# Half of the MLP's down tiles leave PSUM by ScalarE and are summed in DRAM by GpSimd's accumulating DMAs

## The chip, the cores and the metric

One core of a Trainium2 chip. The metric is the device time of one execution in microseconds; the time of a kernel is the median over its runs.

## The reference

With x of 2048 tokens x 576 channels in fp32, two branches are computed and added to x:

```
xn  = layernorm(x)
A   = attention(xn @ wqkv) @ wo        # 32 heads of 18; each token looks at itself and
                                       # 7 earlier tokens, 2 apart (window 8, dilation 2)
h   = gelu(layernorm(xn) @ w1)
hs  = shift(h) @ w2                    # four channel groups shifted by +1, -1, +2, -2 tokens
x1  = xn + hs
B   = x1 + gelu(layernorm(x1) @ w3) @ w4   # w3: 576 x 4608, w4: 4608 x 576
out = x + A + B
```

GELU is the tanh form. Everything has to come out at fp32 accuracy.

## The kernel before, in words

All matmuls run in the fp32r type. Each operand is split into a high and a low part (`split_w`, `split_x`: ScalarE makes the high part by a cast, VectorE the low part by a subtraction), and a product is made of high x high, high x low and low x high. So the 576 input channels become the 14 pairs of 128 rows in `PAIRS`.

The program is written out by hand in one order for each engine. `Y`, 16 tiles of 128 tokens x 576 in SBUF, holds xn, then x1, then the running sum. The stages are: the qkv projection (q, k and v are spilled to DRAM), the token mixing with w1 and w2, the MLP with attention beside it, and at the end the output projection with wo.

The MLP is a loop over 72 units `(c, b)`: 18 chunks of 256 hidden channels, and in each of them 4 blocks of 512 tokens. In a unit stand two up tiles, `up(c, b, i)`, 14 matmuls each into a PSUM bank (L676; two such buffers), and then the four down tiles of the unit before, `down(*prev, j)`, 12 matmuls each into a pair of banks (L696; three such buffers, taken in turn). After an up tile ScalarE passes over it twice with GELU, once to `hi` (rounded to fp32r, L680) and once to `g32` (L681), and VectorE makes `lo = g32 - hi` (L682). After a down tile VectorE adds the PSUM pair to `Y[:, t, :]` (L699). Tile t is 4 b + j.

Attention's vector work has no matmuls. It is a generator (`attention`), and `bg(r)` takes some of its VectorE operations (L628, L631, L608, L612) ahead of each up and down tile, by a budget in microseconds that is written in the code, until all is done; what is left at unit 66 is issued there at once. Its sums are written to `od` in DRAM. Between units 4 and 66 `load_xa` and `add_x` add the input x to `Y`, one tile in four units (L757). The weights of the next chunk are loaded by SP into `rawf` and split by `split_w3` and `split_w4` (L167 on ScalarE, L168 on VectorE).

In the last six units (z = u - 72 = -6 to -1) attention's result comes back: `load_o` loads 512 tokens of `od` in four DMAs (L738), `o_turn` transposes them on VectorE (L129, L130), `put` writes them to DRAM (L137, four DMAs), `get` reads them back with the channels on the partitions (L142), and `split_x` splits them. `load_wo` and `split_wo` do the same for wo. After the loop stand the last four down tiles, and then the output projection, tile by tile (L846), with an add to `Y` (L847) and a store (L848).

Every engine works its instructions off in order; SP issues all DMAs in one queue. GpSimd has nothing to do in the loop.

Of the kernel before, what the change touches and what calls it, by code (L numbers as in the profile page):

```python
# [8 lines left out]
F32 = mybir.dt.float32  # L9
F32R = mybir.dt.float32r  # L10
AF = mybir.ActivationFunctionType
ALU = mybir.AluOpType
# [4 lines left out]
S, D, F = 2048, 576, 4608  # L17
NT = S // 128
NB = S // 512
# [9 lines left out]
NCH = NF // C  # L29
HF = D // 2  # L30
# [10 lines left out]
def dram_ap(t, offset, dims):  # L41
    return bass.AP(tensor=t.tensor, offset=t.offset + offset, ap=[list(d) for d in dims])
# [3 lines left out]
def fused_block(ctx, tc, x, wqkv, wo, w1, w2, w3, w4, out):  # L46
    nc = tc.nc
    pe, act, dve, pool, sp = nc.tensor, nc.scalar, nc.vector, nc.gpsimd, nc.sync
# [8 lines left out]
    dram = ctx.enter_context(tc.tile_pool(name="dram", bufs=1, space=DRAM))  # L57

    Y = base.tile([128, NT, D], F32, name="Y")
# [10 lines left out]
    od = dram.tile([S, D], F32, name="od")  # L70
# [56 lines left out]
    def turn(src, t):  # L127
        c = slice(32 * t, 32 * t + 32)
        dve.transpose(ST[:, 4:20, c], src[:, :512].rearrange("p (j c) -> p j c", c=32))  # L129
        dve.transpose(ST[:, 0:4, c].rearrange("p (a j) c -> p a j c", a=2),  # L130
                      src[:, 512:].rearrange("p (j c) -> p j c", c=32)[:, None, :, :]
                      .to_broadcast([128, 2, 2, 32]))

    def put(key):
        xd[key] = dram.tile([5, 128, 512], F32, name="xd", bufs=4)
        for q in range(4):
            sp.dma_start(dram_ap(xd[key], 128 * q, [[512, 32], [32 * 512, 20], [1, 128]]),  # L137
                         ST[32 * q:32 * q + 32])

    def get(key, xt):  # L140
        for k in ((0, 3), (3, 5)):
            sp.dma_start(xt[:, 4 + k[0]:4 + k[1], :].bitcast(F32),  # L142
                         xd[key][k[0]:k[1]].rearrange("k p c -> p k c"))
# [13 lines left out]
    def in_order(blk):  # L157
        return blk.rearrange("p (q t c) -> p t q c", q=4, t=4)

    def by_token(blk):  # L160
        return blk.rearrange("p (t q c) -> p t q c", q=4, t=4)

    def quads(t_, b, q):
        return dram_ap(t_, (512 * b + 128 * q) * D, [[D, 32], [32 * D, 4], [1, D]])

    def split_w(dst_hi, dst_lo, raw):
        act.copy(dst_hi, raw)  # L167
# [353 lines left out]
    def n_turn(t, zpool):  # L521
        z = zpool.tile([128, D], F32, name="rz", tag="rz")
        act.activation(z, Y[:, t, :], AF.Identity, bias=RS[2][:, t, 0:1], scale=RS[2][:, t, 1:2])  # L523
        turn(z, t % 4)
        if t % 4 == 3:
            put(("n", t // 4))
# [5 lines left out]
    for t in range(NT):  # L532
        ps = psb.tile([128, 2, 512], F32, name="ps", tag="b")
# [9 lines left out]
        yv = Y[:, t, :].rearrange("p (h c) -> p h c", h=2)  # L543
        dve.tensor_tensor(yv, ps[:, :, :HF], yv, op=ALU.add)
        stats(Y[:, t, :], 2, t)
        if t in (1, 3):
            f = (t - 1) // 2
# [22 lines left out]
    hp = ctx.enter_context(tc.tile_pool(name="hp", bufs=2, reuse_waits="tile"))  # L570
    tp = ctx.enter_context(tc.tile_pool(name="tp", bufs=1, reuse_waits="tile"))
    room(tp)

    apc = tc.tile_pool(name="ap", bufs=1, reuse_waits="tile")
# [97 lines left out]
    def up(c, b, i):  # L672
        f = c * C + i
        ps = psa.tile([128, 512], F32, name="p1", tag="a")
        for n, (a, w) in enumerate(PAIRS):
            pe.matmul(ps, W3[f][:, w, :], x1n[b][:, a, :], start=n == 0, stop=n == len(PAIRS) - 1)  # L676
        hi = hp.tile([128, 512], F32R, name=f"hi{i}")
        g32 = hp.tile([128, 512], F32, name="g32")
        lo = hp.tile([128, 512], F32R, name=f"lo{i}")
        act.activation(by_token(hi), in_order(ps), AF.Gelu_apprx_tanh)  # L680
        act.activation(by_token(g32), in_order(ps), AF.Gelu_apprx_tanh)  # L681
        dve.tensor_tensor(lo, g32, hi.bitcast(F32), op=ALU.subtract)  # L682
        hid[c, b, i] = (hi, lo)

    def down(c, b, j):
        t = 4 * b + j
        col = slice(j * 128, (j + 1) * 128)
        ps = psb.tile([128, 2, 512], F32, name="ps", tag="b")
        seq = []
        for i in range(C):  # L690
            w = W4[c * C + i]
            hi, lo = hid[c, b, i]
            seq += [(hi, w, 0), (hi, w, 1), (lo, w, 0)]
        for n, (h, w, p) in enumerate(seq):
            for k in range(2):
                pe.matmul(ps[:, k, :HF], h[:, col], w[:, p, k * HF:(k + 1) * HF],  # L696
                          start=n == 0, stop=n == len(seq) - 1)
        yv = Y[:, t, :].rearrange("p (h c) -> p h c", h=2)
        dve.tensor_tensor(yv, ps[:, :, :HF], yv, op=ALU.add)  # L699

    units = [(c, b) for c in range(NCH) for b in range(NB)]
    NU = len(units)
    RATE = [6.1, 6.1, 6.1, 6.1]
    wop = None
    LATE = {(0, 0): (12, 13), (0, 1): (14, 15)}
    Wo = None
    prev = None
    opool = None
# [22 lines left out]

    otile, xagain, xo = {}, {}, {}

    def load_o(b):
        if b < NB:
            otile[b] = opool.tile([128, 4, D], F32, name="ot", bufs=2)
            for q in range(4):
                sp.dma_start(otile[b][32 * q:32 * q + 32], quads(od, b, q))  # L738

    def load_xa(t):  # L740
        xagain[t] = tp.tile([128, D], F32, name="rz", tag="rz")
        sp.dma_start(xagain[t], xf[t * 128:(t + 1) * 128, :])

    def o_turn(b, t):
        turn(otile[b][:, t, :], t)
        if t == 3:
            put(("o", b))

    def o_block(b):
        if b < 2:  # L750
            xo[b] = ring_block(("o", b))
        else:
            xo[b] = xp.tile([128, 9, 512], F32R, name=f"x1n{b}")
        return xo[b]

    def add_x(t):
        dve.tensor_tensor(Y[:, t, :], Y[:, t, :], xagain[t], op=ALU.add)  # L757

    for u, (c, b) in enumerate(units):
        if u == 2:  # L760
            ap_pool = apc.__enter__()
            state["gen"] = attention(ap_pool)
            next(state["gen"])
        r = RATE[b] / 6 if u >= 4 else 0.0
        z = u - NU
        if z == -6:
            while not state["done"]:
                bg(1e9)
            open_wo()
            load_o(0)  # L770
            load_o(1)
        if z == -4:
            load_wo(0)
        if z == -3:
            split_wo(0)
            load_wo(2)
        if z == -2:
            load_wo(4)
        if z == -1:
            split_wo(2)  # L780
        for i in range(C):
            bg(r, False)
            up(c, b, i)
            if (u, i) in ((0, 0), (1, 0)):
                get(("n", u + 2), x1n[u + 2])
            for t in LATE.get((u, i), ()):
                n_turn(t, tp)
            if u in (1, 2) and i == 0:
                split_x(x1n[u + 1], 0)
            if z in (-4, -3) and i == 1:  # L790
                get(("o", z + 4), o_block(z + 4))
            if z == -1 and i == 1:
                get(("o", 2), o_block(2))
            if z == -1:
                split_x(xo[1], i)
        if b == 3:
            split_w3(2 * c + 3)
        if prev is not None:
            for j in range(4):
                bg(r, j == 1)  # L800
                down(*prev, j)
                if u in (1, 2) and j == 1:
                    split_x(x1n[u + 1], 1)
                if z in (-5, -4, -2):
                    o_turn({-5: 0, -4: 1, -2: 2}[z], j)
                if z == -1 and j > 1:
                    o_turn(3, 2 * j - 4)
                    o_turn(3, 2 * j - 3)
                if z == -3 and j > 1:
                    split_x(xo[0], j - 2)  # L810
            if z in (-5, -4):
                load_o(z + 7)
        if b == 1:
            split_w3(2 * c + 2)
        if b == 2:
            split_w4(2 * c + 2)
            load_f(2 * c + 4)
        if b == 0 and c > 0:
            split_w4(2 * c + 1)
            load_f(2 * c + 3)  # L820
        if 4 <= u < 4 + 4 * NT:
            if u % 4 == 0:
                load_xa(u // 4 - 1)
            if u % 4 == 2:
                add_x(u // 4 - 1)
        prev = (c, b)
    for j in range(4):
        down(*prev, j)
        if j == 0:
            split_wo(4)  # L830
            get(("o", 3), o_block(3))
        if j > 1:
            split_x(xo[2], j - 2)

    for t in range(NT):
        b, s = divmod(t, 4)
        yv = Y[:, t, :].rearrange("p (h c) -> p h c", h=2)
# [6 lines left out]
        if t < NT - 1:  # L844
            ps = psb.tile([128, 2, 512], F32, name="ps", tag="b")
# [39 lines left out]
```

## Time and profile before

| | |
|---|---|
| median of 3 runs | 1295.52 us (1294.83 to 1296.1) |
| the profiled execution | 1294.73 us |
| its span | 1292.9 us, granted clock 1.000 |
| TensorE, matmul | 1285.0 us busy |
| VectorE | 935.6 us busy |
| ScalarE | 362.0 us busy |
| GpSimd | 38.1 us busy |
| DMA | 125.20 MB, all issued by SP but for instruction fetches |

The span goes from the first to the last instruction of the profiled execution; the execution's own time also holds what lies around it. Busy times are sums of one engine's instructions. An engine that is idle costs nothing unless another one waits for it.

### The profile page before, as it was taken

To read this page: it belongs to the slowest core of one execution; us is meant where nothing else is said; L and a number is where in the kernel's file an instruction comes from. 1 tells how busy PE (TensorE), PEld (TensorE's weight loads), DVE (VectorE), ACT (ScalarE), POOL (GpSimd) and SP (SyncE) were. 2 spreads that over 40 slices of the span, in tenths; PEclk is the share of its full clock that TensorE was granted. 3 is DMA by queue.
4 is the path that set the end of the run, shared out by engine and by line. 5 is a ranking of instruction groups with operands and counts; after the bars stand their busy time and mean duration, and the time that the engine had idled before them with its cause. 6 is when DMAs were issued, how large, how long until landed. Compare 5 with 4: busy or idle time off the path is not lost.

```text
span 1292.9 us, 18505 instructions
## 1 busy us (share of the span) xinstructions
PE 1285.0 (99%) x7678; PEld 1184.8 (92%) x7678; DVE 935.6 (72%) x1336; ACT 362.0 (28%) x601; POOL 38.1 (3%) x108
## 2 busy tenths in 40 slices
PE   8999999999999999999999999999999999999998
PEld 8999998899899999989999999999998999999998
DVE  6455534689576778888878888878888878855741
ACT  3332126524412232232222132232232231213310
POOL 2011100021000000000000000000000000000000
PEclk9999999999999999999999999999999999999999
DMA  7646884346702030221221221221232111156842
GB/s 204 154 122 137 172 174 143 92 108 155 229 29 73 29 101 20 82 75 46 82 73 48 82 72 42 89 73 29 75 99 71 31 49 44 58 120 158 208 145 83
DMA packets 157828, 125.20 MB, mean 97 GB/s; under 512 B 72608, under 2 KB 129824, under 8 KB 157744
## 3 DMA queue, kind: packets, MB, share of 16 engines
q1 hardware_dynamic: 157744, 124.02, 34.9%
q8 instruction: 60, 0.98, 0.3%
q14 instruction: 24, 0.20, 0.0%
HBM read 83.56 MB, written 39.39 MB: 95 GB/s over the span
## 4 chain that ended last, share of the span: by engine, by line
PE 94%; DMA 2%; DVE 2%; ACT 1%; SPq 0%; issue 0%; ACTq 0%
PE ps L696 35%; PE p L676 34%; PE ps L182 17%; PE ps L431 4%; PE ps L276 3%; DMA xd<-st 1%; PE ps L446 1%; PE ps L104 1%; DMA xt<-xd 0%; DMA raw<-in_A_wqkv_dram 0%; DMA x1n<-xd 0%; DVE st L129 0%; SPq L137 0%; PE p L853 0%; ACT rz L523 0%
## 5 line engine op out<-in xcount | busy, mean ns | idle before, releaser
L696 PE MATMUL ps<-W,hi 128*128 128x288 f32 x2304 | 398.7, 294 | 0.5 <-DVE Y L699 0.4
L696 PEld LDWEIGHTS ps<-W,hi 128*128 128x128 f32 x2304 | 339.5, 188 | 7.2 <-DVE Y L699 1.0
L680 ACT ACTIVATE hi<-p 128x512 fp32r<-128x512 f32 x144 | 86.2, 598 | 578.4 <-PE p L676 578.4
L696 PE MATMUL ps<-W,lo 128*128 128x288 f32 x1152 | 245.3, 294 | 0.0
L676 PE MATMUL p<-x1n,W 128*128 128x512 f32 x1008 | 234.6, 389 | 0.0
L676 PE MATMUL p<-xt,W 128*128 128x512 f32 x1008 | 234.4, 389 | 0.0
L676 PEld LDWEIGHTS p<-xt,W 128*128 128x128 f32 x1008 | 187.3, 188 | 36.9
L676 PEld LDWEIGHTS p<-x1n,W 128*128 128x128 f32 x1008 | 187.3, 188 | 36.8
L699 DVE TENSOR_TENSOR Y<-ps,Y 128x576 f32<-128x576 f32 x288 | 212.0, 748 | 11.0 <-PE ps L696 10.7
L682 DVE TENSOR_TENSOR lo<-g,hi 128x512 fp32r<-128x512 f32 x144 | 99.5, 691 | 159.5 <-ACT g L681 159.4
L696 PEld LDWEIGHTS ps<-W,lo 128*128 128x128 f32 x1152 | 185.3, 187 | 0.0
L182 PE MATMUL ps<-WQ,xt 128*128 128x432 f32 x672 | 134.4, 359 | 0.0
L182 PEld LDWEIGHTS ps<-WQ,xt 128*128 128x128 f32 x672 | 125.5, 188 | 5.4
L628 DVE TENSOR_TENSOR prod<-q,k 128x1152 f32<-128x1152 f32 x64 | 86.4, 1349 | 0.0
L631 DVE TENSOR_REDUCE L<-prod 128x64 f32<-128x1152 f32 x64 | 86.1, 1346 | 0.0
L681 ACT ACTIVATE g<-p 128x512 f32<-128x512 f32 x144 | 85.3, 592 | 0.0
L612 DVE TENSOR_TENSOR o<-o,prod 128x1152 f32<-128x1152 f32 x56 | 75.5, 1349 | 0.0
L608 DVE TENSOR_TENSOR prod<-v,L 128x1152 f32<-128x1152 f32 x56 | 75.5, 1348 | 0.0
L167 ACT CAST W<-rawf 128x640 fp32r<-128x640 f32 x72 | 50.3, 700 | 70.5 <-PE ps L696 69.2
L168 DVE TENSOR_TENSOR W<-rawf,W 128x640 fp32r<-128x640 f32 x72 | 56.2, 783 | 0.0
L182 PE MATMUL ps<-W,h 128*128 128x288 f32 x384 | 53.5, 295 | 0.0
L182 PEld LDWEIGHTS ps<-W,h 128*128 128x128 f32 x384 | 51.9, 188 | 0.1
(108 smaller groups left out, 888.7 us busy)
## 6 DMA issues: line engine op xcount, KB each, us to landing
xd<-st SPq DMA_DIRECT2D x48, 320.0 KB, 6.0
qkvd<-stg SPq DMA_DIRECT2D x24, 432.0 KB, 3.6
rawf<-in_B_w_dram SPq DMA_DIRECT2D x36, 288.0 KB, 3.2
rawf<-in_B_w_dram SPq DMA_DIRECT2D x36, 256.0 KB, 3.0
xt<-xd SPq DMA_DIRECT2D x8, 768.0 KB, 5.1
xin<-in_A_x_dram SPq DMA_DIRECT2D x16, 288.0 KB, 3.8
q<-qkvd SPq DMA_DIRECT2D x8, 576.0 KB, 4.0
k<-qkvd SPq DMA_DIRECT2D x8, 576.0 KB, 5.0
```

The source lines that it names most:

```text
L168: dve.tensor_tensor(dst_lo, raw, dst_hi.bitcast(F32), op=ALU.subtract)
L182: pe.matmul(ps[:, h, :n], xs(a), ws(b, h), start=i == 0, stop=i == len(PAIRS) - 1)
L608: dve.tensor_tensor(dst, vv, Lf[:, :, w:w + 1].to_broadcast([128, TPP * GH, HD]), op=ALU.mult)
L612: dve.tensor_tensor(o, o, dst, op=ALU.add)
L628: dve.tensor_tensor(prod.rearrange("p (j h) d -> p j (h d)", h=GH), q, k[:, r0:r0 + TPP, :], op=ALU.mult)
L631: dve.tensor_reduce(Lf[:, :, w], prod, axis=AX.X, op=ALU.add)
L676: pe.matmul(ps, W3[f][:, w, :], x1n[b][:, a, :], start=n == 0, stop=n == len(PAIRS) - 1)
L680: act.activation(by_token(hi), in_order(ps), AF.Gelu_apprx_tanh)
L681: act.activation(by_token(g32), in_order(ps), AF.Gelu_apprx_tanh)
L682: dve.tensor_tensor(lo, g32, hi.bitcast(F32), op=ALU.subtract)
L696: pe.matmul(ps[:, k, :HF], h[:, col], w[:, p, k * HF:(k + 1) * HF], start=n == 0, stop=n == len(seq) - 1)
L699: dve.tensor_tensor(yv, ps[:, :, :HF], yv, op=ALU.add)
```

## The change

In the first 17 chunks the down tiles with j = 1 and j = 3 are no longer added to `Y` by VectorE. ScalarE copies the PSUM pair to a tile `ev` in SBUF (two buffers), and GpSimd issues a DMA that writes it to a tensor `yd[t]` in DRAM in the first chunk and adds it there in the next sixteen. In the last chunk all tiles are added by VectorE as before. From unit z = -4 on, SP loads two of the eight `yd` tiles a unit, into the same `ev` buffers, and one unit later VectorE adds them to `Y` (`load_yd`, `add_yd`); those of tiles 13 and 15 are added after the last down tile.

To make room in SBUF, `g32` has one buffer in place of two; the tile of `load_xa` and `n_turn` moves to attention's pool, which is opened earlier; `load_xa` and `add_x` stand two units earlier; and attention's result is loaded in halves of 256 tokens (three buffers of two tiles) in place of blocks of 512 (two buffers of four).

```diff
-    def quads(t_, b, q):
-        return dram_ap(t_, (512 * b + 128 * q) * D, [[D, 32], [32 * D, 4], [1, D]])
+    def quads(t_, b, q, h):
+        return dram_ap(t_, (512 * b + 128 * q + 64 * h) * D, [[D, 32], [32 * D, 2], [1, D]])
...
-        g32 = hp.tile([128, 512], F32, name="g32")
+        g32 = hp.tile([128, 512], F32, name="g32", bufs=1)
...
         yv = Y[:, t, :].rearrange("p (h c) -> p h c", h=2)
-        dve.tensor_tensor(yv, ps[:, :, :HF], yv, op=ALU.add)
+        if j in BYDMA and c < NCH - 1:
+            e = ep.tile([128, 2, HF], F32, name="ev", bufs=2)
+            act.copy(e, ps[:, :, :HF])
+            pool.dma_start(yd[t], e.rearrange("p h c -> p (h c)"),
+                           accum_op=ALU.add if c else ALU.bypass)
+        else:
+            dve.tensor_tensor(yv, ps[:, :, :HF], yv, op=ALU.add)
+
+    BYDMA = (1, 3)
+    yd = {t: dram.tile([128, D], F32, name=f"yd{t}") for t in range(NT) if t % 4 in BYDMA}
+    ep = ctx.enter_context(tc.tile_pool(name="ep", bufs=1, reuse_waits="tile"))
...
-    def load_o(b):
-        if b < NB:
-            otile[b] = opool.tile([128, 4, D], F32, name="ot", bufs=2)
-            for q in range(4):
-                sp.dma_start(otile[b][32 * q:32 * q + 32], quads(od, b, q))
+    def load_o(b, h):
+        otile[b, h] = opool.tile([128, 2, D], F32, name="ot", bufs=3)
+        for q in range(4):
+            sp.dma_start(otile[b, h][32 * q:32 * q + 32], quads(od, b, q, h))
...
     def load_xa(t):
-        xagain[t] = tp.tile([128, D], F32, name="rz", tag="rz")
+        xagain[t] = ap_pool.tile([128, D], F32, name="rz", tag="rz")
...
     def o_turn(b, t):
-        turn(otile[b][:, t, :], t)
+        turn(otile[b, t // 2][:, t % 2, :], t)
...
+    def load_yd(t):
+        xagain[t] = ep.tile([128, D], F32, name="ev", bufs=2)
+        sp.dma_start(xagain[t], yd[t])
+
+    def add_yd(t):
+        dve.tensor_tensor(Y[:, t, :], Y[:, t, :], xagain[t], op=ALU.add)
...
-            load_o(0)
-            load_o(1)
+            load_o(0, 0)
+            load_o(0, 1)
+            load_o(1, 0)
...
                 if z in (-5, -4, -2):
                     o_turn({-5: 0, -4: 1, -2: 2}[z], j)
+                    if j % 2 and (z, j) != (-2, 3):
+                        load_o(*{-5: ((1, 1), (2, 0)), -4: ((2, 1), (3, 0)), -2: ((3, 1),)}[z][j // 2])
...
-            if z in (-5, -4):
-                load_o(z + 7)
...
-        if 4 <= u < 4 + 4 * NT:
+        if 2 <= u < 2 + 4 * NT:
+            if u % 4 == 2:
+                load_xa(u // 4)
             if u % 4 == 0:
-                load_xa(u // 4 - 1)
-            if u % 4 == 2:
                 add_x(u // 4 - 1)
+        for j in BYDMA:
+            if z >= -3:
+                add_yd(4 * z + 12 + j)
+            if z >= -4:
+                load_yd(4 * z + 16 + j)
         prev = (c, b)
     for j in range(4):
         down(*prev, j)
...
+        if j == 3:
+            add_yd(13)
+            add_yd(15)
```

More of the change, by code (lines that the diff above doesn't have):

```diff
@@ L704, in fused_block @@
     wop = None
+    ap_pool = apc.__enter__()
     LATE = {(0, 0): (12, 13), (0, 1): (14, 15)}
@@ L760, in fused_block @@
         if u == 2:
-            ap_pool = apc.__enter__()
             state["gen"] = attention(ap_pool)
@@ L786, in fused_block @@
             for t in LATE.get((u, i), ()):
-                n_turn(t, tp)
+                n_turn(t, ap_pool)
             if u in (1, 2) and i == 0:
```

## The prediction

> **What bounds the kernel now.** I read the page's head and busy rows first, then the waits of TensorE, then windows of four units (one chunk of the MLP) over the long middle, then the chain of waits there, then the timeline of the end. The page, and after the dots three rows of the view of DMA issues (KB each, median us from issue to landing):
>
> ```profile
> span 1292.9 us, 18505 instructions
> PE 1285.0 (99%) x7678; PEld 1184.8 (92%) x7678; DVE 935.6 (72%) x1336; ACT 362.0 (28%) x601; POOL 38.1 (3%) x108
> L699 DVE TENSOR_TENSOR Y<-ps,Y 128x576 f32<-128x576 f32 x288 | 212.0, 748 | 11.0 <-PE ps L696 10.7
> xd<-st SPq DMA_DIRECT2D x48, 320.0 KB, 6.0
> ...
> rz<-in_A_x_dram SPq DMA_DIRECT2D x16, 288.0 KB, 3.3
> out_dram<-Y SPq DMA_DIRECT2D x15, 288.0 KB, 2.1
> rawf<-in_A_wo_dram SPq DMA_DIRECT2D x2, 144.0 KB, 9.5
> ```
>
> TensorE is busy for 1285.0 of 1292.9 us; only 7.9 us of the whole span are not its own. The change takes work from VectorE (72%), which is not what sets the end. A busy TensorE can hide waits inside its pipeline, so I looked for them: the waits of TensorE from 300 to 460 us, two windows of four units each (columns: stretch, its length, busy PE, PEld, DVE, ACT, POOL, clock, DMA share, GB/s) and the chain of waits (start, length, what).
>
> ```profile
> PE ps L696 <- DVE Y L699: 0.4, 1, 0.4
> ...
> 709.10:760.00 50.90, 50.90 (x306) 46.44 (x306) 43.02 (x49) 11.15 (x20) 0.00 (x0) 1.00 0.24 67
> 912.63:963.51 50.88, 50.88 (x306) 46.44 (x306) 42.83 (x52) 14.35 (x23) 0.00 (x0) 1.00 0.19 63
> ...
> 696.40 6.34 PE ps L696 x48
> 702.74 6.36 PE p L676 x28
> 709.10 6.44 PE ps L696 x48
> ```
>
> Two up tiles take 6.36 us and four down tiles 6.34, so a unit is 12.70 us and four are 50.80; the windows measure 50.90 and 50.88 at full clock. The missing 0.1 us is in the one unit in four whose downs take 6.44. Nothing else is hidden in this stage: the loop goes at the rate of its matmuls.
>
> **The change part by part.** *Down tiles.* 18 chunks x 4 blocks x 4 tiles are the 288 adds of L699. In 17 chunks, two tiles of four leave by ScalarE: 136 adds go from VectorE, 136 x 0.748 = 102 us of busy time. TensorE waited for these adds 0.4 us once, and for the 0.1 us per chunk. Where is that? The timeline of the unit at 709.10:
>
> ```profile
> 707.23 0.69 DVE L682 TENSOR_TENSOR lo<-g,hi 128x512 fp32r<-128x512 f32 x1
> 709.63 0.59 ACT L681 ACTIVATE g<-p 128x512 f32<-128x512 f32 x1
> 710.25 0.69 DVE L682 TENSOR_TENSOR lo<-g,hi 128x512 fp32r<-128x512 f32 x1 [1.07 <-ACT g L681]
> 710.87 0.82 DVE L168 TENSOR_TENSOR W<-rawf,W 128x640 fp32r<-128x640 f32 x1
> 711.61 1.35 DVE L608 TENSOR_TENSOR prod<-v,L 128x1152 f32<-128x1152 f32 x1
> 712.88 0.75 DVE L699 TENSOR_TENSOR Y<-ps,Y 128x576 f32<-128x576 f32 x1
> 713.69 0.80 PE L696 MATMUL ps<-W,hi 128*128 128x288 f32 x4
> ```
>
> The add of tile j=0 ends at 713.63 and tile j=3, which takes over its PSUM pair (three pairs), starts at 713.69 with a matmul group of 0.80. What makes it late is ahead of it on VectorE (lo, the W3 split, an attention step), a row that begins by waiting for ScalarE, so no backlog of earlier adds. j=0 stays on VectorE and nothing ahead of it goes: gain 0. If I am wrong, the gain is 18 x 0.1 + 0.4 = 2.2 us, the end below nothing.
>
> *ScalarE copies.* No copy of 576 columns is in the trace; two other forms bound it:
>
> ```profile
> L286 ACT COPY stg<-ps 128x864 f32<-128x864 f32 x24 | 21.2, 882 | 102.4 <-PE ps L182 55.9 <-issue 41.8 <-DMA xt<-xd 4.6
> L279 ACT COPY stg<-ps 128x288 f32<-128x288 f32 x12 | 4.8, 400 | 10.7 <-PE ps L276 9.8 <-ACT WQ L167 0.9
> ```
>
> Half way between, 0.64 us; two a unit are 1.3 us beside 2.8 to 3.6 (11.15 and 14.35 over four units). Each waits for its down tile, and behind it on ScalarE stand the W4 cast, attention's exp and the next unit's two GELUs. A down takes 6.34 / 4 = 1.585 us. The pair of j=1 goes to the next unit's j=0 and that of j=3 to the next unit's j=2; each of them is wanted again after two downs and two ups, 2 x 1.585 + 6.36 = 9.5 us, of which the copy takes 0.64. The next GELU comes one up tile after the last down, 3.18 us, by when the copy of j=3 is long over. So ScalarE has room: 0.
>
> *One g32 buffer in place of two.* The second GELU pass must now wait for the subtraction of the one before: it ends at 707.92, the pass starts at 709.63. 1.7 us to spare: 0.
>
> *GpSimd's accumulating DMAs.* GpSimd is idle through the loop (0.00 in both windows), so waiting there blocks no one. What can block is the two-deep buffer ev: a copy needs the DMA of one unit earlier to have read it. With a unit of 12.70 and a copy of 0.64, that loop (wait, issue, read-add-write of 288 KB, receipt) has 12.06 us. The trace has no such DMA. Nearest rows: a store of 288 KB lands in 2.1 us, a load of 288 KB in 3.3; the slowest rows are 6.0 for a store and 9.5 for a load under load. So from 2.1 (a store) to 15.5 (9.5 + 6.0). I take 5.4 (2.1 + 3.3), as sizes and row length are those of these two rows: less than half of 12.06, cost 0. The Trainium skill, "DMA: Bandwidth & Descriptors", Anatomy of one DMA, fits a GpSimd-issued DMA by 2.0 us plus bytes over 436 GB/s, an estimate of 2.7 us here; by it the sum is the same.
>
> *Earlier load_xa/add_x* move by two units with one VectorE op of 0.75; TensorE waits for neither: 0. *o in halves:* 16 SP issues more, behind them on SP the puts and gets of o; o is wanted by the output projection at 1230.3, and each half frees its buffer sooner: 0.
>
> *The end.* Eight adds of yd come back on VectorE, and eight loads on SP. Rows of the last units:
>
> ```profile
> 1199.18 0.39 SPq L722 DMA_DIRECT2D rawf<-in_A_wo_dram  x1
> ...
> 1206.83 0.75 DVE L699 TENSOR_TENSOR Y<-ps,Y 128x576 f32<-128x576 f32 x1
> 1209.66 0.69 PE L696 MATMUL ps<-W,hi 128*128 128x288 f32 x4
> ...
> 1212.94 1.32 DVE L168 TENSOR_TENSOR Wo<-rawf,Wo 128x1152 fp32r<-128x1152 f32 x1
> 1215.74 0.69 DVE L682 TENSOR_TENSOR lo<-g,hi 128x512 fp32r<-128x512 f32 x1 [1.49 <-ACT g L681]
> ...
> 1227.07 0.72 DVE L699 TENSOR_TENSOR Y<-ps,Y 128x576 f32<-128x576 f32 x1
> 1228.37 1.41 DVE L699 TENSOR_TENSOR Y<-ps,Y 128x576 f32<-128x576 f32 x2
> 1228.70 0.69 PE L696 MATMUL ps<-W,hi 128*128 128x288 f32 x4
> 1230.29 29.77 PE L182 MATMUL ps<-Wo,xt 128*128 128x288 f32 x224
> ```
>
> Two adds in a row take 1.41 us (the x2 row). Tiles 1 and 3 are added ahead of the lo's of the unit at 1204.9, tiles 5 and 7 at 1212.94, where VectorE then has 1.49 us idle: hidden by that idle time, with 0.1 to spare. Tiles 9 and 11 stand directly ahead of the add at 1227.07, whose row names no idle time before it. That add then ends at 1227.79 + 1.41 = 1229.20, and the last down, which needs its pair at 1228.70, starts 0.5 us late; with the hand-over of 0.06 seen at 713.63, **0.6 us**. All after it on TensorE (the output projection at 1230.29) moves by that. Tiles 13 and 15 follow behind the last downs, where projection tiles of 3.7 us (29.77 / 8) give VectorE room: 0.
>
> **Sum.** The profiled execution took 1294.73 us, 1.83 more than its span; the median of the three runs is 1295.52, 0.79 higher. 1294.73 + 0.6 = 1295.3 for a profiled one, 1295.52 + 0.6 = **1296.1** for the median. I expect no measurable change: about 0.2% (2.6 us) is what a measurement of this kernel can tell from none.
>
> **Rivals.** *The ev loop is longer than a unit.* Decides from 12.06 us on. ScalarE then holds every unit back: at 15.5 us a unit is 16.14, over 67 units +230 us, about 1526. For: the operation isn't in the trace and reads, adds and writes in DRAM. Against: both rows of its size add to 5.4, the DMA share in the loop is 0.2. Chance 0.08.
>
> *GpSimd can build its DMAs only while VectorE pauses.* VectorE pauses 50.90 - 43.02 = 7.9 us in four units, mostly ahead of the lo's, in the up half. A DMA of j=1 or j=3 then waits through the rest of the downs and an up, 8 us at worst, and the loop takes 5.4 + 8 = 13.4: +1.3 x 67 = 90 us, 1386. The Trainium skill, "SBUF — State Buffer", section "SBUF: two separate sides", says so for two-port operations of VectorE (copies and scalar operations in fp32), which starve GpSimd's descriptor writing. Against: VectorE's rows in this loop are two-input adds and multiplies, and reduces. No run so far shows it. Chance 0.03.
>
> *The yd loads come back late.* On SP they stand behind the put and the load of o; issued at about 1200 after the row at 1199.18, they land at 1203.6 (3.3), and the add at 1206.83 is not moved. If a load takes 9.5 us, as the slowest row, it lands at 1209.8; two adds, two lo's (0.69 each) and the add of j=0 end at 1213.3, 3.6 us after 1209.66: with the 0.6, 1299.7. If two of the four boundaries do so, 1303. For: the puts fill the queue there. Against: load rows of this size are at 3.3. Decides from landing 3 us later than I take. Chance 0.14.
>
> *Less backlog on VectorE removes the small stalls:* -2.2 + 0.6, 1293.9, still no measurable change. To be faster by 2.6 us a third of all TensorE's idle time would have to go, and most of that is ahead of the loop: 0.05. *The change doesn't do what it says:* the last chunk's tiles stay on VectorE by the condition in the diff; I see nothing that undoes it.
>
> **Numbers.** No measurable change 0.70 (the forecast, and small stalls either way); slower 0.25 (0.08 + 0.03 + 0.14); faster 0.05. The range goes from 1293.5 (the stalls gone, and the spread of the runs) to 1304 (two late boundaries); left out are the two loop rivals and the rest of the faster case, some 0.15.
>
> **What would show it.** Right: four-unit windows of 50.9 us again; L699 x152 and 136 copies of about 0.64 us; VectorE down by some 95 us of busy time (102 less 8 x 0.75); a wait of TensorE for the add of j=0 of 0.5 us near 1229. Wrong: units over 12.7 us with ScalarE's copy waiting for a DMA (the loop); VectorE waiting for loads into ev near 1202 or 1213 and TensorE behind it (late loads); a span that is the same beside a longer time (cost outside).

## The result, and the profile after

The changed kernel takes 1297.51 us (median of 12 runs, 1296.33 to 1299.12) against 1294.87 for the kernel before beside it: 1.0022 times as long, with a 95% interval of 1.0014 to 1.0030. That is 2.6 us slower. The forecast was 1296.1 us and no measurable change. The time lies inside the range and, by the ratio, just past the line of 0.2% that the prediction drew (0.22%), and the interval leaves no change out. Small as it is, the loss is clear of the noise, and it is a sum of larger pieces of both signs. The forecast stood on a median of three runs, 1295.52, which is 0.65 above the median of 12; the 0.6 that it added to the kernel before is to be held against the 2.6.

The page of the changed kernel (parts 1, 3, 5 and 6; the add of L699 is now L705, the copy L701, GpSimd's DMA L702, `add_yd` L771):

```profile
span 1296.2 us, 19061 instructions
PE 1284.3 (99%) x7678; PEld 1184.0 (91%) x7678; DVE 857.8 (66%) x1208; ACT 447.4 (35%) x737; POOL 154.5 (12%) x244
...
q0 software_dynamic: 19072, 40.12, 22.4%
...
L701 ACT COPY ev<-ps 128x576 f32<-128x576 f32 x136 | 87.1, 640 | 276.4 <-PE ps L696 275.8
L705 DVE TENSOR_TENSOR Y<-ps,Y 128x576 f32<-128x576 f32 x152 | 113.5, 750 | 9.4 <-PE ps L696 9.4
...
yd<-ev POOLq DMA_DIRECT2D x136, 288.0 KB, 4.3
```

The change did what it says: 152 adds are left on VectorE, 136 copies of 640 ns stand on ScalarE, and each DMA lands 4.3 us after its issue. VectorE lost 78 us of busy time (the prediction had 95), and the kernel got nothing for it. Its rows add up to 92 us less: the adds fall from 212.0 to 113.5, `add_yd` brings 5.7, the rest is small. The other 14 are overlap: rows that stand back to back overlap (in the prediction's timeline the row at 711.61 ends at 712.96, and the next begins at 712.88), and busy time counts such time once.

TensorE's busy time is the same within 1 us, so the 3.3 us that the span of the profiled execution grew are waits. The view of TensorE's waits from 300 us on (us in total, times, longest):

```profile
PE ps L696 <- DVE Y L705: 2.1, 3, 0.8
PE ps L696 <- ACT ev L701: 1.8, 2, 0.9
```

Before, the same view had one wait of 0.4. Now there are five. In the timeline of TensorE they are the five groups that name what they waited for (start, length, what, idle time and its end):

```profile
344.77 0.80 PE L696 MATMUL ps<-W,hi 128*128 128x288 f32 x4 [0.95 <-ACT ev L701]
1108.01 0.80 PE L696 MATMUL ps<-W,hi 128*128 128x288 f32 x4 [0.84 <-ACT ev L701]
1197.68 0.80 PE L696 MATMUL ps<-W,hi 128*128 128x288 f32 x4 [0.52 <-DVE Y L705]
1211.43 0.80 PE L696 MATMUL ps<-W,hi 128*128 128x288 f32 x4 [0.79 <-DVE Y L705]
1231.59 0.80 PE L696 MATMUL ps<-W,hi 128*128 128x288 f32 x4 [0.82 <-DVE Y L705]
```

In between, the loop is faster than before. Four units at the place of the window shown in the prediction, and a later four:

```profile
708.58:759.38 50.80, 50.80 (x306) 46.40 (x306) 38.19 (x40) 16.21 (x28) 6.97 (x8) 1.00 0.57 115
911.86:962.66 50.80, 50.80 (x306) 46.40 (x305) 38.77 (x43) 19.30 (x31) 6.98 (x8) 1.00 0.63 134
```

50.80 instead of 50.90 and 50.88: the 0.1 us per chunk is gone here. Before, 12 units of the loop took 12.79 to 12.85 us in place of 12.70; after, one does. The DMA engines' share is 0.57 and 0.63 instead of 0.24 and 0.19.

Taking the starts of the units from both timelines, the 3.0 us by which the output projection starts later (1233.29 against 1230.29) add up like this:

| stretch | before, us | after, us | difference |
|---|---|---|---|
| to the third unit of the MLP | 333.42 | 332.56 | -0.9 |
| third unit (stall at 344.77) | 13.06 | 13.91 | +0.85 |
| the 65 other units of the loop together | 826.67 | 825.62 | -1.05 |
| unit with the stall at 1108.01 | 12.70 | 13.80 | +1.1 |
| unit z = -3 (1197.68) | 12.70 | 13.48 | +0.8 |
| unit z = -2 (1211.43) | 12.69 | 13.76 | +1.1 |
| last unit and last down tiles (1231.59) | 19.05 | 20.16 | +1.1 |

The five stalls are 4.9 us, the gains 1.9. Of the first row 0.7 is in the first two units (19.09 against 19.76); the other 0.2 lies ahead of the MLP, whose start differs by more than that between kernels that are alike up to there (312.96 in e1, 313.36 in e2).

How a late DMA reaches TensorE is best seen at 1108. The timeline of all engines there:

```profile
1104.83 1.36 DVE L608 TENSOR_TENSOR o<-v,L 128x1152 f32<-128x1152 f32 x1 [6.61 <-DMA v<-qkvd]
1106.11 0.68 DVE L682 TENSOR_TENSOR lo<-g,hi 128x512 fp32r<-128x512 f32 x1
1106.83 0.60 ACT L681 ACTIVATE g<-p 128x512 f32<-128x512 f32 x1 [3.77 <-DVE lo L682]
1107.32 0.63 ACT L701 COPY ev<-ps 128x576 f32<-128x576 f32 x1
1108.58 0.75 DVE L705 TENSOR_TENSOR Y<-ps,Y 128x576 f32<-128x576 f32 x1
```

VectorE waits 6.6 us for attention's v (2.2 at the same place before). SP needs longer to issue that load, 3.29 us against 1.28, and from the start of the issue to VectorE's start it is 9.4 us against 6.2 (the first two rows are the kernel before):

```profile
1096.37 1.28 SPq L587 DMA_DIRECT2D v<-qkvd  x1
1102.53 1.36 DVE L608 TENSOR_TENSOR o<-v,L 128x1152 f32<-128x1152 f32 x1 [2.16 <-DMA v<-qkvd]
...
1095.40 3.29 SPq L587 DMA_DIRECT2D v<-qkvd  x1
```

Behind that wait stands `lo` of the first up tile. The second GELU pass of the next up tile needs the one g32 buffer and waits for that `lo`; behind the GELU on ScalarE stands the copy of j=1; and TensorE starts at 1108.01, right behind the end of the copy (1107.95) and ahead of the add of j=0 (1108.58). So this tile j=3 took the pair of j=1, not that of j=0: the pairs no longer go strictly in turn. Which pair a tile gets is fixed when the program is built; that the builder expects ScalarE's copy to free one early is my reading, which no run shows.

At 344.77 a `put`, beside GpSimd's first DMA, lands later: the `get` that waits for it leaves 10.25 us after the put's start, 8.74 before. ScalarE's wait for that `get` grows from 2.1 to 4.0 us, and GELU and the copy stand behind it (the first two rows are the kernel before):

```profile
335.07 0.91 SPq L142 DMA_DIRECT2D x1n<-xd  x2
339.99 0.62 ACT L148 CAST rt<-x1n 64x512 fp32r<-64x512 f32 x1 [2.12 <-DMA x1n<-xd]
...
336.39 0.91 SPq L142 DMA_DIRECT2D x1n<-xd  x2
341.02 0.62 ACT L148 CAST rt<-x1n 64x512 fp32r<-64x512 f32 x1 [3.99 <-DMA x1n<-xd]
344.10 0.62 ACT L701 COPY ev<-ps 128x576 f32<-128x576 f32 x1
```

At 1197.68 the row of wo lands 0.6 us later (ScalarE's cast of it at 1192.45 instead of 1191.86), and again the second GELU waits for `lo`. Why that row is late no run separates: with the same DMAs the stall comes in e2 and not in e9. The stalls of the last units in the timeline:

```profile
1189.85 9.89 SPq L137 DMA_DIRECT2D xd<-st  x4
1199.78 2.86 SPq L748 DMA_DIRECT2D ot<-od  x4
1202.86 0.91 SPq L768 DMA_DIRECT2D ev<-yd  x2
...
1207.26 1.48 DVE L771 TENSOR_TENSOR Y<-Y,ev 128x576 f32<-128x576 f32 x2 [4.53 <-DMA ev<-yd]
1209.38 0.60 ACT L681 ACTIVATE g<-p 128x512 f32<-128x512 f32 x1 [2.86 <-DVE lo L682]
1210.62 0.75 DVE L705 TENSOR_TENSOR Y<-ps,Y 128x576 f32<-128x576 f32 x1
...
1229.48 1.38 DVE L771 TENSOR_TENSOR Y<-Y,ev 128x576 f32<-128x576 f32 x2
1230.79 0.75 DVE L705 TENSOR_TENSOR Y<-ps,Y 128x576 f32<-128x576 f32 x1
```

The put takes SP 9.9 us to issue (6.58 before, and 6.80 with copies only, e1, where o comes in halves too; so it is the DMAs that slow it). So the loads of yd leave at 1202.86, VectorE waits 4.5 us for them, `lo`, the GELU that waits for it and the add of j=0 follow, and the add ends at 1211.37. At 1229.48 two adds stand directly ahead of the add that frees the pair, as the prediction had it.

### The profile page after: what moved, and what is told of

It reads as the page before. It is cut to its first block, busy times and chain, and to the rows that moved or that the text cites. A ratio compares the mean times of both kernels' runs of the same rounds, so it can differ in the third digit from the quotient of the medians.

```text
span 1296.2 us, 19061 instructions
## 1 busy us (share of the span) xinstructions
PE 1284.3 (99%) x7678; PEld 1184.0 (91%) x7678; DVE 857.8 (66%) x1208; ACT 447.4 (35%) x737; POOL 154.5 (12%) x244
## 3 DMA queue, kind: packets, MB, share of 16 engines
q0 software_dynamic: 19072, 40.12, 22.4%
## 4 chain that ended last, share of the span: by engine, by line
PE 91%; DMA 4%; DVE 2%; issue 1%; SPq 1%; ACT 1%; DVEq 0%; ACTq 0%
PE p L676 33%; PE ps L696 31%; PE ps L182 19%; PE ps L431 4%; PE ps L276 3%; DMA xt<-xd 1%; DMA v<-qkvd 1%; DMA xd<-st 1%; PE ps L446 1%; PE ps L104 1%; DVE st L129 0%; DMA raw<-in_A_wqkv_dram 0%; DMA ev<-yd 0%; DMA x1n<-xd 0%; DVE Y L705 0%
## 5 line engine op out<-in xcount | busy, mean ns | idle before, releaser
L702 POOL DMA_DIRECT2D yd<-ev x136 | 116.2, 855 | 754.0 <-ACT ev L701 754.0
L701 ACT COPY ev<-ps 128x576 f32<-128x576 f32 x136 | 87.1, 640 | 276.4 <-PE ps L696 275.8
L705 DVE TENSOR_TENSOR Y<-ps,Y 128x576 f32<-128x576 f32 x152 | 113.5, 750 | 9.4 <-PE ps L696 9.4
L89 POOL TENSOR_TENSOR rs<-rs,mhalf 128x1 f32<-128x1 f32 x48 | 31.1, 647 | 254.0 <-DVE rs L88 148.4
```

Source lines behind the costliest of these rows:

```text
L701: act.copy(e, ps[:, :, :HF])
L702: pool.dma_start(yd[t], e.rearrange("p h c -> p (h c)"), accum_op=ALU.add if c else ALU.bypass)
```

## The experiments

All are timed in five rounds beside the kernel before on the same chip; the ratios are to that kernel, with 95% intervals. The kernel before had medians of 1294.47 to 1294.62 in them, and 1294.87 beside the changed kernel. So where a time is set against the changed kernel's 1297.51, the difference is 0.25 to 0.4 us less if each is taken against its own kernel before.

**Copies only** (e1): no DMAs by GpSimd, nothing brought back.

```diff
             act.copy(e, ps[:, :, :HF])
-            pool.dma_start(yd[t], e.rearrange("p h c -> p (h c)"),
-                           accum_op=ALU.add if c else ALU.bypass)
...                            # and no load_yd, no add_yd
```

> Changed kernel without GpSimd's DMAs and without the yd loads and adds (half of the down sums of 17 chunks are left out). My theory: the copies cost TensorE nothing and free PSUM pairs sooner, so the 0.1 us stalls of the loop go (-1.3) and so does the one of 0.7 in the second unit, and no stall of 0.7 to 1.1 is left near 345, 1108, 1197, 1211 or 1231 us: 1292.9 us, 2.0 under the kernel before. Rival 1, the copies in ScalarE's order make the stalls: about 1297, as the changed kernel.

Measured: 1292.77 us, 0.9984 (0.9975 to 0.9993). The view of TensorE's waits from 300 us on is empty. Rival 1 falls: copies by ScalarE cost nothing and even gain 1.9 us. The earlier `load_xa`, o in halves and the single g32 buffer are in this run too, and no wait of TensorE shows them costing anything by themselves.

**No way back** (e2): with the accumulating DMAs, without `load_yd` and `add_yd`.

> Changed kernel with GpSimd's accumulating DMAs, but the sums are not brought back (no load_yd, no add_yd; half of the down sums of 17 chunks are missing from the output). My theory: the two stalls at 1211 and 1231 us go (-2.1), those at 345, 1108 and 1197 stay: 1295.4 us. Rival 2, the end alone costs all: 1294.9 or less, with nothing left at 345 and 1108. Rival 3, the DMAs cost outside the span or all along the loop: 1297.5.

Measured: 1295.21 us, 1.0006 (0.9997 to 1.0015). TensorE's waits near 345, 1108 and 1197 stand in its trace, those at 1211 and 1231 are gone. Against copies only, the DMAs alone cost 2.4 us; against the changed kernel, the way back costs 2.3 (2.05 by the kernels before beside them). Rivals 2 and 3 fall, since the loss is neither all at the end nor spread over the loop.

**Two buffers of g32 again** (e3), with attention's mask in bf16 to make room.

```diff
-        g32 = hp.tile([128, 512], F32, name="g32", bufs=1)
+        g32 = hp.tile([128, 512], F32, name="g32")
...
-        mask = ap.tile([128, TPP, GH, W], F32, name="mask")
+        mask = ap.tile([128, TPP, GH, W], mybir.dt.bfloat16, name="mask")
```

> Changed kernel with two buffers of g32 again (the mask of attention is held in bf16 to make room). My theory: where VectorE is held up by a late DMA, the second GELU and the copy behind it on ScalarE no longer wait for lo, so the stalls at 1108 (1.1), 1197 (0.7) and most of that at 1211 (0.7 of 1.0) go; those at 345 and 1231 stay: 1295.1 us. Rival 4, late DMAs cost by themselves and g32 has nothing to do with it: 1297.5, stalls unchanged.

Measured: 1294.98 us, 1.0001 (0.9992 to 1.0010). In size as expected, rival 4 falls. In the trace the stalls at 1108 and 1197 are gone. A part of the expectation missed: that of the next unit shrank little (0.87 against 1.06), and its profiled execution, which at 1297.11 us lies above its median, had waits of 1.30 us at 1223.59 and 0.53 us at 1230.72, in the last unit and the last down tiles, where the yd loads came late once more. The stall near 345 stayed. The mask in bf16 changes nothing that shows: the operation on it takes 0.68 us either way.

**One buffer of g32 in the kernel before** (e4).

```diff
-        g32 = hp.tile([128, 512], F32, name="g32")
+        g32 = hp.tile([128, 512], F32, name="g32", bufs=1)
```

> Kernel before with one buffer of g32, nothing else. My theory: the single buffer costs only where a DMA holds VectorE up, and in the kernel before these waits are short: at most 0.1 us near 1197, so 1294.9 to 1295.1. Rival 5, the single buffer costs by itself: 1296 to 1297.5.

Measured: 1294.50 us, 1.0002 (0.9993 to 1.0011), 0.4 under the expected range and level with the kernel before. In its trace the unit near 1197 takes 12.89 us in place of 12.70, and nothing else is longer by more than 0.1. The single buffer costs next to nothing where no DMA holds VectorE up for long (rival 5 falls); in the changed kernel it costs 2.5 (e3; 2.3 by the kernels before). There it takes both, the late DMAs and the single buffer.

**Copies only, the PSUM pairs strictly in turn** (e5).

```diff
+    def pair():
+        npair[0] += 1
+        return psb.tile([128, 2, 512], F32, name="ps", tag=f"b{npair[0] % 3}", bufs=1)
...                            # in all stages:
-        ps = psb.tile([128, 2, 512], F32, name="ps", tag="b")
+        ps = pair()
```

> The run with copies only (no DMAs, no sums brought back: half of the down sums of 17 chunks are left out), with the three PSUM pairs taken strictly in turn. My theory: in the changed kernel many a tile j=3 takes over the pair of j=1, which ScalarE frees early, and not that of j=0; with the pairs in turn it waits for VectorE's add of j=0 again, so the stall of 0.1 us per chunk (1.3) and part of the 0.7 in the first units come back: 1294.0 to 1294.8 us. Rival 6, it is VectorE's shorter queue that takes the stalls away, whichever pair is used: 1292.8 as with copies only.

Measured: 1294.53 us, 1.0001 (0.9992 to 1.0009). 1.8 us more than with copies only. The wait of 0.5 us for the add of j=0 is back in the view of TensorE's waits, the first two units take 19.82 us (19.09 in e1), and 12 units take 12.79 to 12.85 as in the kernel before. Rival 6 falls: the gain of the change comes from which pair a tile takes over, not from VectorE's shorter queue.

**The kernel before, with the W3 split after j=0** (e7).

```diff
-        if b == 3:
-            split_w3(2 * c + 3)
...
                 down(*prev, j)
+                if b == 3 and j == 0:
+                    split_w3(2 * c + 3)
```

> Kernel before, with split_w3 of the fourth unit of a chunk issued after the down tile j=0 instead of ahead of it. My theory: the add of j=0 then stands 0.74 us earlier on VectorE and the stall of 0.1 us per chunk goes: 1293.2 us (-1.4). Rival: those 0.1 us are no wait for the add of j=0: 1294.6, no change.

Measured: 1293.18 us, 0.9990 (0.9981 to 0.9999); four units in its loop are 50.80 us. So the 0.1 us per chunk was the wait for the add of j=0, and it goes by an order of issue as well.

**Copy, and add on VectorE at once** (e8), the version that the first runs point to.

```diff
             act.copy(e, ps[:, :, :HF])
-            pool.dma_start(yd[t], e.rearrange("p h c -> p (h c)"),
-                           accum_op=ALU.add if c else ALU.bypass)
+            dve.tensor_tensor(yv, e, yv, op=ALU.add)
...                            # and no load_yd, no add_yd
```

> Changed kernel with ScalarE's copies, but VectorE adds the copy to Y at once (no GpSimd DMAs, no yd, same sums as the reference). My theory: what helps in the change is the PSUM pair that ScalarE frees early, and what costs is the DMAs and the way back; this keeps the one without the other: 1292.8 to 1293.2 us, faster than both kernels. Rival: VectorE's queue, now as long as before, brings the stalls back: 1294.6.

Measured: 1292.45 us, 0.9984 (0.9976 to 0.9993), 0.35 under the expected range, level with copies only (1292.77) and faster than both kernels. The head of its page:

```profile
span 1290.4 us, 18772 instructions
PE 1283.4 (99%) x7678; PEld 1184.3 (92%) x7678; DVE 938.1 (73%) x1336; ACT 447.5 (35%) x737; POOL 38.1 (3%) x108
```

VectorE is as busy as in the kernel before (935.6 us), and yet the view of TensorE's waits from 300 us on is empty. VectorE's busy time did not decide the time.

**The sums brought back in the projection** (e9): `load_yd` of tiles 1 and 3 in the last unit, then tile by tile.

```diff
+        if s in BYDMA:
+            add_yd(t)
+            if t + 4 < NT:
+                load_yd(t + 4)
```

> Changed kernel with the yd sums brought back tile by tile in the output projection (load of tiles 1 and 3 in the last unit, add ahead of the tile's projection add, then the load of the tile four further). My theory: the stalls at 1211 and 1231 us go, those at 345, 1108 and 1197 stay, and the projection hides the adds: 1295.3 us. Rival: the adds and loads hold up the projection's own adds and stores: 1297 or more.

Measured: 1295.14 us, 1.0004 (0.9995 to 1.0013), as without a way back (1295.21): the projection hides all eight adds. The unit at 1096 still has its stall (0.8 us), and so has the one near 345; that at 1197, which was expected to stay, is not in its trace.

**Both cures** (e10): e3 and e9 together.

> Changed kernel with two g32 buffers (mask in bf16) and the yd sums brought back in the projection. My theory: only the stall at 345 us (0.9 to 1.4, a late put and get with ScalarE's copy behind it) is left of the five, and the two cures add up: 1293.2 to 1294.2 us, level with or under the kernel before. Rival: one cure takes the other's place, as both act in the last units: 1295.1.

Measured: 1294.31 us, 0.9997 (0.9988 to 1.0006), 0.1 over the expected range. In its trace one wait is left, at 344 us. Its profiled execution took 1293.43, 0.9 under the median, so most runs lose more than this trace shows. The cures add up less than in full: 2.5 and 2.4 us alone, 3.2 together, so a part of them is likely the same stalls.

**One ev buffer** (e11), without the way back.

```diff
-            e = ep.tile([128, 2, HF], F32, name="ev", bufs=2)
+            e = ep.tile([128, 2, HF], F32, name="ev", bufs=1)
```

> The run without the way back (half of the down sums of 17 chunks missing), with one ev buffer instead of two. The copy of j=3 must now wait until the DMA of j=1 has landed: 0.4 to the issue + 0.87 + 4.3, against the 2.5 us that lie between the copies. My theory: ScalarE waits some 2.8 us a unit and TensorE still hardly waits, as the pair of j=3 is wanted only 9.5 us later and the next GELU has room: 1295 to 1297 us. Rival: the loop over ev is near its limit and the units grow with it, by a good part of 2.8 us each: 1340 or more.

Measured: 1302.50 us (5 runs), 1.0064 (1.0052 to 1.0077). A miss on both sides: 7.3 us more than with two buffers, far from 1340, but well over 1297. ScalarE's view of waits and two copies of one unit in its timeline:

```profile
ACT ev L701 <- DMA yd<-ev: 361.9, 81, 9.3
...
701.18 0.64 ACT L701 COPY ev<-ps 128x576 f32<-128x576 f32 x1 [2.08 <-PE ps L696]
706.52 0.64 ACT L701 COPY ev<-ps 128x576 f32<-128x576 f32 x1 [4.70 <-DMA yd<-ev]
```

The loop over ev is 4.7 us from the end of a copy to the start of the next, so with two buffers some 7 us of the 12.06 are to spare. With one, most units keep their 12.70, but the GELUs and casts behind the waiting copy have no slack left, and single units lose 0.3 to 3.7 us, the unit at 1189.71, where wo is split, most.

**Plain writes in place of accumulating ones** (e12), without the way back.

```diff
-                           accum_op=ALU.add if c else ALU.bypass)
+                           accum_op=ALU.bypass)
```

> The run without the way back, with plain writes in place of accumulating ones (same bytes from SBUF; the sums are left out). My theory: the share of the DMA engines falls, the load of v near 1100 us lands sooner and the stall there gets shorter or goes; the stall at 345 stays, as its writes are plain already: 1294.0 to 1295.0 us against 1295.2. Rival: what delays the other DMAs is the number of GpSimd's DMAs and not the adding: 1295.2, the same stalls.

Measured: 1293.82 us, 0.9993 (0.9984 to 1.0001), 0.2 under the expected range and 1.4 less than with accumulating (runs from 1293.09 to 1294.39 against 1294.78 to 1297.03 in e2). Its DMA queues, its own writes and the one wait left:

```profile
q0 software_dynamic: 10880, 40.12, 8.3%
yd<-ev POOLq DMA_DIRECT2D x136, 288.0 KB, 2.4
PE ps L696 <- ACT ev L701: 1.2, 1, 1.2
```

The same bytes take 8.3% of the DMA engines instead of 22.0% (e2), and land in 2.4 us instead of 4.3. The stall near 1100 is gone, the one near 345, where the first chunk writes plainly in all these kernels, stays. The rival falls: in the loop it is the adding, not the number of DMAs or their bytes, that delays the others; SP's issue of the v load near 1095 takes 1.34 us again (3.23 in e2). The 2.4 us of e2 over copies only thus fall into 1.05 for plain DMAs (e12 against e1), about the size of the stall near 345, and 1.4 for the adding. That `put` near 345 is late with plain DMAs as well (10.34 us from its start to the `get`, 8.74 in e1). What in a DMA holds up the others, the shared DMA engines or something else, no run separates.

## Why the prediction was right or wrong

- **The bound.** Right. TensorE sets the time, and 78 us taken from VectorE brought nothing; e8 shows it from the other side.
- **Gain of the small stalls, put at 0.** Wrong, and the lower bound (-2.2) was near: 1.9 us were gained (e1). The step that failed is that tile j=3 takes over the pair of j=0, read rightly from the timeline of before and carried over to after. Where evictions differ between engines, the pair is chosen otherwise, and j=3 waits for a copy that comes early (e5).
- **Copies at 0.** The duration (0.64 us, measured 0.640) and the cost of the copies by themselves were right (e1). What I named as queued behind the copy was right; I did not ask what stands ahead of it on ScalarE and may wait: the GELU that waits for g32, and the cast that waits for a `get`.
- **One g32 buffer at 0, 1.7 us to spare.** This step failed. The spare time was read where no DMA was late. In the kernel before it holds (e4); beside the late DMAs it cost 2.5 us (e3). That overlaps with the cost of the DMAs below, since the stalls at 1108 and 1197 need both.
- **The accumulating DMA.** Mis-sized a little: 5.4 taken, 4.3 measured, far under 12.06, so the rival of the ev loop and that of the starved GpSimd did not come about; the loop took 4.7 us (e11). Waits of GpSimd's DMAs for VectorE's pauses do not show in this loop either: DMAs of 4.3 us, with GpSimd held never longer than 0.90 us by one, beside a VectorE that is busy 38 of 50.8 us. By the rule of the Trainium skill, "SBUF — State Buffer", section "SBUF: two separate sides", they would have come with VectorE's two-port operations; the two-input adds of this loop did not bring them. But the cost of such a DMA to others was not in the sum at all. It takes 22% of the DMA engines' time, and v's load lands 8.8 us after its issue instead of 6.2. The DMAs cost TensorE 2.4 us (e2 against e1), 1.4 of them by the adding (e2 against e12) and 1.05 by plain DMAs already (e12 against e1).
- **The end.** The mechanism was right: the adds of tiles 9 and 11 ahead of the add of j=0 held TensorE for 1.1 us, where I had 0.6. The other 0.5 is VectorE coming later to them: its transposes start 12.50 us after the last unit (1225.63 against 1213.13), 11.99 before (1223.23 against 1211.24).
- **Late yd loads**, a rival at 0.14, came about at one boundary (1211.43), by the put that holds SP, and cost 1.1 us where I had priced 3.6 (0.9 with two buffers of g32, e3). The order of the cause, SP's put ahead of the loads, was as named.
- **The sum.** +0.6 forecast, +2.6 measured: five stalls of 4.9 against gains of 1.9 in the profiled execution, and 0.3 behind the start of the projection. The forecast of no measurable change is missed by a hair (0.22% against the line of 0.2%); the direction is slower. That the time came out inside the range is in part luck: of the five stalls only the last was in the sum, one more was a rival, three were at nothing, and a gain that was at nothing as well took 1.9 us off again.

## What to carry to other kernels

Before taking work from an engine, look whether TensorE waits for it at all; here the only part that gained anything was that a PSUM pair came free early, which a copy by ScalarE gives without any DMA. A buffer count that looks to have slack should be checked at the units where a DMA is late, not at a typical one, since one wait runs on through all in-order engines. Sums that come back at the end belong where the engines have idle time, here the output projection, and not ahead of the operation that frees TensorE's next buffer.

## What the runs showed of the hardware

An accumulating DMA of 288 KB issued by GpSimd lands in 4.3 us at the median (2.4 to 9.5, the eight plain writes of the first chunk among them), against 2.4 as a plain write, and takes 22.0% against 8.3% of the DMA engines for the same 40.12 MB, 2.7 times as much; the packets are 19072 against 10880. GpSimd was busy 0.87 us with each at the median, against 0.54 for a plain one. Beside the accumulating DMAs the loads of v landed in 8.8 us in place of 6.2, and loads of 256 KB of weights in 4.2 in place of 3.0.
